# Attention's two products in plain float32, two small matmuls side by side in the array, in a one-core kernel of attention and two MoE layers

## The chip, the core and the metric

One NeuronCore of one Trainium2 chip runs the whole program in one launch. TensorE is called PE below (PEld is its weight load), VectorE DVE, ScalarE ACT, GpSimd POOL, and SyncE SP; SP issues nearly all transfers. The metric is the device time of one execution in microseconds (us), smaller is better, as the median of three runs.

## What is computed

Inputs are float32. Attention has 4 batches of 8 heads, 576 positions and 64 numbers a head; its output, 4 x 576 x 512, goes through two layers of a gated kind.

```python
def _attn_ref(q, k, v, s):
    scores = scale * np.matmul(q, k.transpose(0, 1, 3, 2))
    s_pos = np.maximum(s, 0.0)
    cum = np.cumsum(s_pos, axis=-1)
    bias = -(cum[:, :, :, None] - cum[:, :, None, :])
    scores = np.where(causal, -1000000000.0, scores + np.minimum(bias, 0.0))
    scores = scores - np.max(scores, axis=-1, keepdims=True)
    attn = np.exp(scores)
    attn = attn / (np.sum(attn, axis=-1, keepdims=True) + 1e-09)
    return np.matmul(attn, v).astype(np.float32)
...
x = attn_out.transpose(0, 2, 1, 3).reshape(B, S, H * D)
x = _moe_ref(x=x, **moe_kwargs)        # two products with w_in, a norm, one over positions with w_sg, one with w_out
return _moe2_ref(x=x, **moe2_kwargs)   # the same with other weights, relu in place of gelu, and no residual
```

## The kernel before

**Two number formats.** A float32 matmul has two forms here. The plain form is issued as two matmuls of all its columns. The other, float32r in the program and `fp32r` in the profile's rows where it is written, is one matmul, but with a rounded operand; to keep precision the kernel splits an operand into a rounded high part and the rest as a low part, and adds the products of the parts. The MoE layers (`plan_moe`, lines 284 to 523) work in parts throughout, and the change leaves them alone.

**Attention of a pair of heads** (two heads share 128 partitions, 64 each). `ldqk` loads q and k, `transposes` (lines 588 to 612) transposes them on PE (lines 596, 597) and splits the result: ACT writes the high parts (lines 608, 610), DVE the low parts (lines 609, 611). `stack` (614 to 625) then copies parts between partitions by transfers on SP, so that one 128-row product holds two part products: for each head two transfers make `qk` (622, 623), one makes the rows of `own` (624), and one brings the cumulated bias (617).

**Attention of a head** (`plan_head`, from 637). Steps S0 to S4 make the scores of five blocks of queries, in six pieces of 64, 192, 320, 448, 288 and 288 columns; each piece is two float32r matmuls (665), one with `qk` and one with `own` (66 rows: a part product and the bias). DVE masks a piece and takes the row minimum (670), ACT takes the exponential and its sum (674). N0 and N1: POOL adds 1e-9 and takes the reciprocal (681, 682) and scales the blocks (181, a helper). X0 to X3: PE transposes the blocks, 15 matmuls a head (727); ACT writes the rounded high part (736), DVE the low part (737). V0 to V3: for each of eight pieces, 1,600 columns in all, the values' product with the high part and with the low part (756). F0 and F1: ACT and DVE add the two halves of the sum (767, 768).

Six of the 32 heads (those with a 1 in `FULL`, line 56) do the values' product in the plain form instead (754), without low parts and with 64 weight columns, and the first pair's scores are plain too (`NQ`, line 58).

**Order.** A `Plan` holds all steps with a place (a head's number plus an offset of a table such as `HEAD`, line 35) and the steps they come after; it emits the steps in order of place, and a scheduler sets the order on each engine at build time. Each engine runs its list in that order. In the first batch there is no MoE work yet; `keep_busy` (lines 139, 820) puts 80 matmuls on zeros into that stretch, whose results nobody reads. The second layer comes behind the last attention (`late`).

Of the kernel before, what the change touches and what calls it, by code (L numbers as in the profile page):

```python
# [30 lines left out]
PA, PM, XB, NA = 6, 2, 3, 0  # L31

PAIR = {"ldqk": -6.63, "ldv": -4.33, "T": -2.16, "K": -4.2}
PAIR0 = {"ldqk": -1.63, "ldv": 0.61, "T": -6.3, "K": -6.13}
HEAD = {"S0": -1.3, "S1": -5.8, "S2": -3.15, "N0": -7.58, "S3": -2.18, "S4": -0.16, "N1": -2.11, "vs": 0.99,
        "X0": 0.5, "V0": -2.31, "X1": 0.53, "V1": -2.26, "X2": 0.21, "F0": 1.5, "X3": 1.38, "V2": -10.3,
        "V3": -2.32, "F1": 0.25}
HEAD0 = {"S0": -5.47, "S1": -2.29, "S2": -0.96, "N0": 0.24, "S3": -0.61, "S4": -0.21, "N1": 0.61, "vs": 1.03,
         "X0": -0.04, "V0": -3.06, "X1": -1.37, "V1": -2.52, "X2": 1.1, "F0": 1.62, "X3": 1.21, "V2": -4.61,
         "V3": -1.47, "F1": 1.82}  # L40

MOE = {"Va": (1.47, 2.25), "Vb": (-5.19, 8.0), "Vc": (-11.42, 14.73), "U": (3.8, 4.73), "ZY": (6.72, 5.81)}
WEIGHT = {"wv": (-1.41, 2.86), "wu": (8.16, 1.39), "sg": (3.51, 5.66), "wo": (10.07, 5.02)}
MOE2 = {"Va": (-14.18, 0.19), "Vb": (6.98, 8.23), "Vc": (-0.41, 3.39), "U": (7.05, 7.22), "ZY": (6.41, 19.75)}
WEIGHT2 = {"wv": (-3.82, 8.35), "wu": (9.3, 7.45), "sg": (13.98, 11.05), "wo": (0.84, 2.8)}

MORE = {"t2": 10.21, "d2": 5.99, "sp": 2.89, "sp2": -7.16, "cut": 1.74, "xr": -19.84, "w0": 11, "wn": 20,
        "ws": -1.0, "wd": 0.4, "wk": 4}


ENG = {"n0": "PPP.", "n1": "PPP.", "vshi": "AAD.", "vslo": "PPD.", "wlo": "PPDP", "wmin": "DPPP", "whi": "ADDD",
       "xhi": "DDAA", "xlo": "PPPP", "xdh": "...A", "xdl": "PPPP", "vn": "...D", "vhi": "...D", "vlo": "...P",
       "ghi": "ADPA", "glo": "DPDP", "mu": "PDPD", "var": "PDPD", "xc": "DAA.", "rg": "...D", "tq": "ADD.",
       "tk": "DAD.", "fc": "DAD.", "vc": "DPD.", "vcl": "DPP.", "vdup": "ADA.", "rc": "PPP."}

FULL = "00000100110001000000000000110000"

NQ = 1


def fl(ap):
    return ap.bitcast(F32)
# [35 lines left out]
def attention_two_moe_kernel(  # L98
# [433 lines left out]
    raw_v = ap.tile([128, NB, 2, D], F32, name="raw_v")  # L532
    nc.gpsimd.memset(raw_v[64:128, NT], 0.0)
# [7 lines left out]
    mx = [ap.tile([128, NB], F32, name=f"mx{i}") for i in range(2)]  # L541
    sm_ = [ap.tile([128, NB], F32, name=f"sum{i}") for i in range(2)]
# [5 lines left out]
    own_ = [ap.tile([D + 2, 2, S], F32R, name=f"own{i}") for i in range(2)]  # L548
    for t in own_:
        nc.vector.memset(fl(t[0:D]), 0.0)  # L550
        nc.vector.memset(fl(t[D:, 0]), 1.0)

    def cumulate():
# [11 lines left out]
        for e in range(2):  # L565
            nc.sync.dma_start(out=fl(own_[e][D:, 1]), in_=fl(ch[e:e + 1]))
# [8 lines left out]
    def plan_pair(plan, n, st):  # L575

        b, j = divmod(n, H // 2)
        full = n < NQ

        def ldqk():  # L580

            st["qk4"] = ap.tile([128, 4 * S], F32, tag="qk4", name="qk4")

            r = st["qk4"][:, :(2 * NT + 1) * 2 * D].rearrange("p (t e d) -> p t e d", t=2 * NT + 1, e=2)
# [29 lines left out]
        def stack(e):  # L614
# [3 lines left out]
            if full:  # L618
                return
# [328 lines left out]
```

## Time and profile before

| what | us |
|---|---|
| median of 3 runs (724.37 to 726.17) | 724.9 |
| the profiled execution: device time | 725.51 |
| its span, first to last instruction | 723.7 |
| PE busy (94% of the span), DVE, POOL, ACT | 678.8, 447.8, 393.9, 386.5 |

The profile has the busy time of each engine, a row of tenths for 40 equal slices of the span, groups of instructions by line and shape, who waited for whom, and instructions in order of time. A matmul's length in it runs until its result is written and overlaps the next; what it costs in a dense run is the distance from its start to the next start. Stages below are by time from the span's start: stage 1, 0 to 125 us (the first eight heads and the first layer's weights), stage 2, 125 to 425 (attention with the first layer), stage 3, from 425 (the end of the first layer and the second).

### The profile page before, as it was taken

The numbers are of one execution on the slowest core, as the hardware profiler recorded it, in microseconds if no ns is written. First come the engines' busy times: TensorE is split into PE (matmuls) and PEld (weight loads), VectorE is DVE, ScalarE is ACT, GpSimd is POOL, SyncE is SP. The second block draws the span as 40 slices with busy tenths as digits, with TensorE's granted clock in tenths as the row PEclk, the third lists the DMA queues.
The fourth block names the chain that finished last, engine by engine and source line by source line (L and its number), as shares of the span: only waits on it lengthen the run. The fifth ranks groups of instructions, "written<-read, shape, count | busy, mean of one in ns | idle before, by whom it ended". The sixth has DMA issues, their size and how long they took to land.

```text
span 723.7 us, 13198 instructions
## 1 busy us (share of the span) xinstructions
PE 678.8 (94%) x4377; PEld 604.1 (83%) x4377; DVE 447.8 (62%) x1191; ACT 386.5 (53%) x1002; POOL 393.9 (54%) x601
## 2 busy tenths in 40 slices
PE   9887888898999998989999999989889999999997
PEld 4476767678889998989979998979888998988996
DVE  8876767788568887766976749985871202402111
ACT  3675557888655876655876544543442414313321
POOL 4754747876474794476563546586674416413211
PEclk9998778999999999999999999999999999999999
DMA  8567677755566465466466053435521001010011
GB/s 210 144 160 173 175 164 156 190 138 124 116 149 153 99 169 119 103 152 154 95 161 140 18 164 84 142 110 187 167 84 52 0 30 46 2 44 30 0 47 57
DMA packets 94396, 81.60 MB, mean 113 GB/s; under 512 B 64116, under 2 KB 72308, under 8 KB 94328
## 3 DMA queue, kind: packets, MB, share of 16 engines
q1 hardware_dynamic: 93128, 80.46, 44.3%
q8 instruction: 35, 0.57, 0.3%
q10 hardware_dynamic: 1200, 0.30, 0.2%
q14 instruction: 33, 0.27, 0.1%
HBM read 39.87 MB, written 14.30 MB: 75 GB/s over the span
## 4 chain that ended last, share of the span: by engine, by line
PE 45%; DMA 6%; DVE 6%; POOL 2%; issue 2%; ACT 1%; SPq 1%; DVEq 0%; POOLq 0%; ACTq 0%
DMA stage<-in_moe_w_in_dram 3%; PE pp L727 3%; PE acc L756 2%; PE s L665 2%; PE pb L472 2%; PE pb L432 2%; PE pb L431 2%; PE pb L430 2%; PE pb L473 2%; PE pb L474 2%; PE pm L404 2%; PE pb L325 1%; PE pb L328 1%; PE pb L326 1%; PE pm L406 1%
## 5 line engine op out<-in xcount | busy, mean ns | idle before, releaser
L674 ACT ACTIVATE p<-p,mx 128x320 f32<-128x320 f32 (+4 forms) x160 | 89.6, 561 | 29.7 <-DVE mx L670 28.8
L181 POOL TENSOR_SCALAR p<-p,sum 128x448 f32<-128x448 f32 (+4 forms) x160 | 90.1, 575 | 4.9
L441 POOL TENSOR_TENSOR g<-u,g 128x256 fp32r<-128x256 f32 (+1 forms) x40 | 32.0, 805 | 94.7 <-ACT g L174 89.5
L727 PE MATMUL pp<-idf,p 128*128 128x128 f32 x480 | 78.7, 286 | 4.7 <-POOL p L181 4.5
L670 DVE CUSTOM_DVE_ANT_0 p<-s,mask 128x320 f32<-128x320 f32 (+4 forms) x160 | 66.1, 421 | 20.6 <-PE s L665 17.1
L436 DVE TENSOR_TENSOR u<-u,pb 128x320 f32<-128x320 f32 (+1 forms) x33 | 14.6, 451 | 95.9 <-PE pb L435 95.9
L665 PE MATMUL s<-qk 128*64 128x64 f32 (+7 forms) x204 | 64.1, 351 | 7.8 <-DMA qk<-qk 3.4
L737 DVE TENSOR_TENSOR pl<-pp,ph 128x320 fp32r<-128x320 f32 (+1 forms) x104 | 58.0, 566 | 14.4 <-ACT ph L736 9.0
L727 PEld LDWEIGHTS pp<-idf,p 128*128 128x128 f32 x480 | 57.8, 145 | 10.4 <-POOL p L181 5.2
L736 ACT CAST ph<-pp 128x320 fp32r<-128x320 f32 (+1 forms) x104 | 49.5, 490 | 28.1 <-PE pp L727 21.2
L681 POOL TENSOR_SCALAR sum<-sum 128x3 f32<-128x3 f32 (+1 forms) x64 | 17.0, 266 | 73.6 <-ACT p L674 70.6
L665 PE MATMUL s<-own 66*64 66x64 f32 (+3 forms) x192 | 55.8, 311 | 0.0
L682 POOL TENSOR_TENSOR sum<-sum,minus_one 128x3 f32<-128x3 f32 (+1 forms) x64 | 53.9, 843 | 3.3
L665 PEld LDWEIGHTS s<-qk 128*128 128x128 f32 (+3 forms) x204 | 36.3, 190 | 13.9 <-issue 5.9
L756 PE MATMUL acc<-ph,vs 128*128 128x320 f32 (+1 forms) x208 | 42.9, 289 | 4.8 <-ACT ph L736 2.8
L756 PE MATMUL acc<-pl,vs 128*128 128x320 f32 (+1 forms) x208 | 44.4, 297 | 0.2
L279 POOL TENSOR_TENSOR xl<-x,xh 128x576 fp32r<-128x576 f32 x24 | 35.2, 1479 | 15.6 <-ACT xh L174 12.7
L756 PEld LDWEIGHTS acc<-ph,vs 128*128 128x128 f32 x208 | 34.8, 200 | 8.2 <-ACT ph L736 4.2
L430 PE MATMUL pb<-sgh,vh 128*128 128x320 f32 (+1 forms) x132 | 39.4, 299 | 0.0
L431 PE MATMUL pb<-sgl,vh 128*128 128x320 f32 (+1 forms) x132 | 39.3, 298 | 0.0
L174 ACT CAST g<-u 128x256 fp32r<-128x256 f32 (+1 forms) x40 | 16.9, 432 | 41.8 <-DVE u L436 41.8
L404 PE MATMUL pm<-xh,inh 128*128 128x320 f32 (+1 forms) x124 | 38.3, 309 | 0.7 <-DVE u L275 0.7
(270 smaller groups left out, 2285.7 us busy)
## 6 DMA issues: line engine op xcount, KB each, us to landing
qk<-qk SPq DMA_DIRECT2D x60, 288.0 KB
own<-qk SPq DMA_DIRECT2D x30, 288.0 KB
x_d<-x SPq DMA_DIRECT2D x16, 288.0 KB
x<-x_d SPq DMA_DIRECT2D x16, 288.0 KB
qk<-in_q_dram SPq DMA_DIRECT2D x32, 128.0 KB
stage<-in_moe_w_in_dram SPq DMA_DIRECT2D x8, 512.0 KB
raw_v<-in_v_dram SPq DMA_DIRECT2D x32, 128.0 KB
stage<-in_moe_w_in_dram SPq DMA_DIRECT2D x16, 256.0 KB
```

The lines of the kernel that those rows point to most:

```text
L181: e.tensor_scalar(t, t, by, 1.0, ALU.mult, ALU.mult)
L404: nc.tensor.matmul(pu, W["inh"][:, kk, f], xh[:, kk, c], start=(kk == 0), stop=False)
L430: nc.tensor.matmul(pz, vh[sb][:, f], W["sgh"][:, sb, c], start=(sb == 0), stop=False)
L431: nc.tensor.matmul(pz, vh[sb][:, f], W["sgl"][:, sb, c], start=False, stop=False)
L665: nc.tensor.matmul(pp, a[:, qc], c[:, kc], start=c is first[1], stop=c is not first[1])
L670: nc.vector.tensor_tensor_reduce(out=p, in0=pp, in1=mask[:m, d0 + kc.start:d0 + kc.stop], scale=-0.125, scalar=3e38 if j == 0 else mxt[:m, ...
L674: nc.scalar.activation(p, p, AF.Exp, bias=mxt[:m, i:i + 1], scale=-1.0, accum_out=smt[:m, i:i + 1])
L682: nc.gpsimd.tensor_tensor(smt[:, c], smt[:, c], minus_one[:, c], ALU.pow)
L727: nc.tensor.transpose(ps[:, w:w + 128], pt[qb][:, kb * 128:kb * 128 + 128], idr if qb == kb and kb else idf)
L736: nc.scalar.copy(hi[:, :w], ps[:, :w])
L737: nc.vector.tensor_tensor(lo[:, :w], ps[:, :w], fl(hi[:, :w]), ALU.subtract)
L756: nc.tensor.matmul(acc, st["vs"][:, kb].rearrange("p a d -> p (a d)"), (hi if part == "hi" else lo)[:, c0:c0 + w], start=first, stop=last)
```

## The change

Scores are plain float32 products of q and k as they come out of the transposes. The two heads of a pair are done in one step: head e uses the array's rows 64 e to 64 e + 63, so its matmul has 64 rows (`rows`), and the two heads write different banks. The bias comes as a further float32r matmul of 64 rows, `ones` with `bias`. There are no parts of q, k, the exponentials or v, and none of the part transfers; the bias rows are still loaded. The values' product is plain for all heads: 12 pieces, with 64 weight columns each, of which 768 columns go to partitions 0 to 63 of the sum (a = 0) and 832 to partitions 64 to 127 (a = 1). One copy follows each group of transposes, and two copies of 64 partitions take the finished sum. The reciprocal moves from POOL to DVE. There are three sets of blocks `pts` for the heads and two buffers of v, and transposes of a head are grouped otherwise (5, 4, 4, 2). The values are one step behind all four groups of transposes. `keep_busy` in the first batch has no matmuls (`wn` 0), and all places are new.

```diff
-MORE = {"t2": 10.21, "d2": 5.99, "sp": 2.89, "sp2": -7.16, "cut": 1.74, "xr": -19.84, "w0": 11, "wn": 20,
...
-FULL = "00000100110001000000000000110000"
-
-NQ = 1
...
+HEAD = {"S2": -2.88, "N0": -0.6, "S4": -1.75, "N1": -0.41, "X0": -0.3, "X1": 0.02, "X2": 0.4, "X3": 0.46,
...
+MORE = {"t2": 10.76, "d2": 6.25, "sp": 2.89, "sp2": -6.56, "cut": 1.6, "xr": -19.03, "w0": 11, "wn": 0,
...
+       "fd": "ADA.", "vc": "DPD.", "vcl": "PPD.", "vdup": "ADA.", "rc": "DDD.", "x0": "DAA.", "x1": "DDD.",
+       "x2": "AAA.", "x3": "DDD."}
...
-    for j in range(2):
+    for j in range(3):
...
+    ones = ap.tile([128, 128], F32R, name="ones")
+    bias = [ap.tile([128, S], F32R, name=f"bias{i}") for i in range(2)]
...
+                copy(key, phase, st["qk"][:, i, c], ps[i])
...
-        def stack(e):
...
-            nc.sync.dma_start(out=fl(t[:D]), in_=fl(parts[:, 0:3:2]))
-            nc.sync.dma_start(out=fl(t[D:]), in_=fl(parts[:, 1:3]))
-            nc.sync.dma_start(out=fl(own_[e][:D]), in_=fl(parts[:, 0:4:3]))
...
+        def scores(i):
...
+            for j, (a, c0, k0, w) in enumerate(PARTS[i]):
+                kc = slice(k0, k0 + w)
+
+                for e in range(2):
+                    rows = slice(D * e, D * e + D)
+                    nc.tensor.matmul(st[a, e][:m, c0:c0 + w], st["qk"][rows, 0, qc], st["qk"][rows, 1, kc], start=True, stop=False)
+                for e in range(2):
+                    rows = slice(D * e, D * e + D)
+                    nc.tensor.matmul(st[a, e][:m, c0:c0 + w], ones[rows, :m], bias[n % 2][rows, kc], start=False, stop=True)
...
+        plan.add(f"S2.{n}", t0 + head["S2"], lambda: [scores(i) for i in range(3)],
+                 [f"T{n}", f"K{n}", f"S4.{n - 1}", f"X3.{2 * n - 2}", f"X3.{2 * n - 3}"])
+        plan.add(f"S4.{n}", t0 + head["S4"], lambda: [scores(i) for i in range(3, NB)], [f"S2.{n}"])
...
+    USE = [(0, 0, 320, 0, 0, 0), (1, 192, 192, 0, 1, 0), (2, 64, 192, 1, 1, 0), (0, 320, 192, 1, 0, 128),
+           (1, 0, 64, 2, 0, 256), (1, 64, 64, 3, 1, 0), (1, 128, 64, 0, 0, 320), (2, 320, 192, 2, 1, 0),
+           (2, 0, 64, 1, 0, 320), (2, 256, 64, 2, 0, 320), (3, 64, 128, 3, 1, 64), (3, 0, 64, 4, 1, 128)]
...
-            nc.scalar.copy(hi[:, :w], ps[:, :w])
-            nc.vector.tensor_tensor(lo[:, :w], ps[:, :w], fl(hi[:, :w]), ALU.subtract)
-            st["x", i] = hi, lo
...
+            copy(f"x{i}", phase, st["x"][i], ps[:, :w])
+
+        def values():
+            st["acc"] = psa.tile([128, 512], F32, tag="a", name="acc")
+
+            for j, (i, c0, w, kb, a, a0) in enumerate(USE):
+                nc.tensor.matmul(st["acc"][64 * a:64 * a + 64, a0:a0 + w], raw_v[m % 2][:, kb, odd], st["x"][i][:, c0:c0 + w],
+                                 start=j in (0, 1), stop=j in (9, 11))
+
+        def finish():
+            x = x_t(h // 2)
+            copy("fc", phase, x[rows, :384], st["acc"][0:64, :384])
+            copy("fd", phase, x[rows, 384:], st["acc"][64:128, :192])
```

In the list of PE before, in the middle of stage 2, the values' product of one head ends and the scores of the next follow (`ph` and `pl` are the high and low parts, `vs` the parts of v; `s` a bank of scores):

```order
L756 MATMUL acc_2669<-pl,vs 128x192
L756 MATMUL acc_2669<-pl,vs 128x64
L756 MATMUL acc_2672<-pl,vs 128x256
L756 MATMUL acc_2672<-ph,vs 128x192
L756 MATMUL acc_2672<-ph,vs 128x64
L756 MATMUL acc_2672<-pl,vs 128x192
L756 MATMUL acc_2672<-pl,vs 128x64
L665 MATMUL s_2727<-qk 128x320
L665 MATMUL s_2727<-own_152 128x320
L665 MATMUL s_2722<-qk 128x448
L665 MATMUL s_2722<-own_152 128x448
```

In the list of PE of the changed kernel, the scores of a pair stand so (`s_1603`, `s_1567` and `s_1577` are the first head's banks, `s_1604`, `s_1568` and `s_1578` the second's; each plain matmul is one row here and two matmuls on the chip):

```order
L617 MATMUL s_1603<-qk 128x288
L620 MATMUL s_1603<-bias_167,ones 128x288
L617 MATMUL s_1604<-qk 128x288
L620 MATMUL s_1604<-bias_167,ones 128x288
L617 MATMUL s_1567<-qk 128x448
L620 MATMUL s_1567<-bias_167,ones 128x448
L617 MATMUL s_1568<-qk 128x448
L620 MATMUL s_1568<-bias_167,ones 128x448
L617 MATMUL s_1577<-qk 128x320
L620 MATMUL s_1577<-bias_167,ones 128x320
L617 MATMUL s_1578<-qk 128x320
L620 MATMUL s_1578<-bias_167,ones 128x320
```

At this place a head's plain product and its bias stand together, and the other head's two come behind them; in other pairs the two plain products stand together and the two biases behind them. The values of a head in the changed list of PE are one run between two groups of transposes (`pt` are the copied transposes):

```order
L688 MATMUL pp<-idf,p_2_139 128x128
L698 MATMUL acc<-pt,raw_v_121 64x320
L698 MATMUL acc<-pt,raw_v_121 64x192 x3
L698 MATMUL acc<-pt,raw_v_121 64x64 x3
L698 MATMUL acc<-pt,raw_v_121 64x192
L698 MATMUL acc<-pt,raw_v_121 64x64 x2
L698 MATMUL acc<-pt,raw_v_121 64x128
```

Over the whole list of PE, matmuls of 64 rows or with 64 weight columns in the plain form come in 100 unbroken runs of one shape in the changed kernel (33 of scores, 18 of the 64-column pieces of scores, 49 of values). Before there are about 25. On SP the list of a pair before is this, all from its first to its last part transfer (`qk_1188` holds the parts):

```order
L617 DMA own_151<-cum_d 2x576
L622 DMA qk<-qk_1188 64x2x576
L623 DMA qk<-qk_1188 64x1152
L624 DMA own_151<-qk_1188 64x2x576
L201 DMA stage<-in_moe_w_out_dram 128x1024
L617 DMA own_152<-cum_d 2x576
L622 DMA qk<-qk_1188 64x2x576
L623 DMA qk<-qk_1188 64x1152
L624 DMA own_152<-qk_1188 64x2x576
```

and after the change, with the loads that stand near it:

```order
L600 DMA bias_167<-cum_d 2x576 x2
L570 DMA raw_v_122<-in_v_dram 128x4x64
L196 DMA stage<-in_moe_w_out_dram 128x1024
L570 DMA raw<-in_q_dram 128x4x64 x2
L571 DMA raw<-in_q_dram 64x2x64
```

Six of the eight transfers of a pair are gone; the two of the bias remain.

## Rows read from the trace of the kernel before

**Rows 1.** The page's line of PE's busy time: us, share of the span, instructions.

```profile
PE 678.8 (94%) x4377; PEld 604.1 (83%) x4377; DVE 447.8 (62%) x1191; ACT 386.5 (53%) x1002; POOL 393.9 (54%) x601
```

**Rows 2.** By stage: PE, PEld, DVE, ACT, POOL busy (instructions), granted clock, DMA share, GB/s.

```profile
0.00:125.00 125.00, 106.87 (x577) 78.08 (x577) 91.78 (x242) 74.26 (x201) 74.29 (x131) 0.88 0.70 169
125.00:425.00 300.00, 285.36 (x2038) 263.47 (x2038) 226.56 (x647) 204.07 (x544) 186.17 (x304) 0.99 0.56 130
425.00:724.00 299.00, 286.55 (x1765) 262.51 (x1764) 129.42 (x303) 108.17 (x258) 133.44 (x166) 0.99 0.24 72
```

**Rows 3.** The same for line 142 alone (only PE, PEld), stage 1.

```profile
0.00:125.00 125.00, 24.80 (x91) 8.79 (x91) 0.88 0.70 169
```

**Rows 4.** DVE in order of time (start, us): last step of heads one and eight.

```profile
43.96 0.41 DVE L768 TENSOR_TENSOR x<-acc,x 64x256 f32<-64x256 f32 x1
...
124.50 0.43 DVE L768 TENSOR_TENSOR x<-acc,x 64x256 f32<-64x256 f32 x1
```

**Rows 5.** Columns as in rows 2: between those two steps, and one stretch in it.

```profile
44.00:124.50 80.50, 66.92 (x381) 55.71 (x381) 57.11 (x165) 50.61 (x143) 49.64 (x79) 0.81 0.68 159
...
62.00:66.00 4.00, 2.48 (x13) 2.49 (x13) 0.49 (x1) 0.52 (x2) 0.00 (x0) 0.50 1.01 226
```

**Rows 6.** PE in order of time (start, us); in brackets idle time before, what ended it.

```profile
63.52 0.61 PE L665 MATMUL s<-qk 128*64 128x64 f32 x2 [2.85 <-DMA qk<-qk]
```

**Rows 7.** PE in order of time: float32r passes in dense runs (weight rows*columns, columns streamed).

```profile
42.12 0.29 PE L665 MATMUL s<-qk 128*128 128x288 f32 x1
42.26 0.30 PE L665 MATMUL s<-own 66*128 66x288 f32 x1
...
147.17 0.37 PE L665 MATMUL s<-qk 128*128 128x448 f32 x1
147.38 0.36 PE L665 MATMUL s<-own 66*128 66x448 f32 x1
```

**Rows 8.** PE in order of time: the first pair's plain scores, one head alone.

```profile
20.63 1.02 PE L665 MATMUL s<-qk 64*128 64x448 f32 x2
21.57 0.47 PE L665 MATMUL s<-own 66*128 66x448 f32 x1
```

**Rows 9.** PE in narrow windows of time: the first pair's plain scores, both heads.

```profile
10.91 0.27 PE L665 MATMUL s<-qk 64*64 64x64 f32 x2
...
11.17 0.60 PE L665 MATMUL s<-qk 64*128 64x192 f32 x4
...
10.91 1.33 PE L665 MATMUL s<-qk 64*64 64x64 f32 x10
12.18 1.04 PE L142 MATMUL idle<-mask 128*128 128x512 bf16 x4
```

**Rows 10.** PE in order of time: a head's first plain values, and what stands around.

```profile
141.91 0.39 PE L326 MATMUL pm<-inl,xh 128*128 128x512 f32 x1
142.13 0.39 PE L328 MATMUL pm<-inh,xl 128*128 128x512 f32 x1
142.45 1.62 PE L754 MATMUL acc<-ph,vs 128*64 128x320 f32 x6
144.00 1.09 PE L727 MATMUL pp<-idf,p 128*128 128x128 f32 x8
```

**Rows 11.** Groups by line: xcount, busy us, mean ns, idle before and who ended it.

```profile
L670 DVE CUSTOM_DVE_ANT_0 p<-s,mask 128x320 f32<-128x320 f32 (+4 forms) x160 | 66.1, 421 | 20.6 <-PE s L665 17.1 <-POOL p L181 1.3 <-PE acc L756 0.5
...
L737 DVE TENSOR_TENSOR pl<-pp,ph 128x320 fp32r<-128x320 f32 (+1 forms) x104 | 58.0, 566 | 14.4 <-ACT ph L736 9.0 <-PE pp L727 2.2 <-PE acc L756 1.8
...
L682 POOL TENSOR_TENSOR sum<-sum,minus_one 128x3 f32<-128x3 f32 (+1 forms) x64 | 53.9, 843 | 3.3
...
L768 DVE TENSOR_TENSOR x<-acc,x 64x320 f32<-64x320 f32 (+1 forms) x52 | 23.3, 452 | 7.3 <-ACT x L767 6.5
...
L670 DVE CUSTOM_DVE_ANT_0 p<-s,mask,mx 128x288 f32<-128x288 f32 x32 | 16.3, 510 | 1.7 <-PE s L665 0.6
...
L670 DVE DVE_READ_ACCUMULATOR2_ANT mx<- 128x1 f32 (+1 forms) x192 | 15.2, 79 | 0.0
```

More of the change, by code (lines that the diff above doesn't have):

```diff
@@ L28 @@
 SIGN = -(1 << 31)
[L31 to L40, printed above, removed]
@@ L627, in plan_pair @@
-        t0, where = 2 * n, PAIR0 if b == 0 else PAIR
-        plan.add(f"ldqk{n}", t0 + where["ldqk"], ldqk, [f"K1.{n - 1}"])
-        plan.add(f"ldv{n}", t0 + where["ldv"], lambda: load(raw_v, v, b, j, raw_v[0:REM, NT]), [f"vs{2 * n - 1}"])
-        plan.add(f"T{n}", t0 + where["T"], transposes,
-                 [f"ldqk{n}", f"K1.{n - 1}"]
-                 + ([f"S{i}.{2 * n - 2}" for i in range(NB)] if full else []))
-        for e in range(2):
-            plan.add(f"K{e}.{n}", t0 + where["K"] if n else -100.0, lambda e=e: stack(e),
-                     [f"T{n}", f"K{1 - e}.{n - 1 + e}"] + [f"S{i}.{2 * n - 2 + e}" for i in range(NB)])
+            st["qk"] = ap.tile([128, 2, S], F32, tag="qk", bufs=2, name="qk")
@@ new lines, in plan_pair @@
+        t0, where, head = 2 * n, PAIR0 if b == 0 else PAIR, HEAD0 if b == 0 else HEAD
+        plan.add(f"ldqk{n}", t0 + where["ldqk"], ldqk, [f"T{n - 1}"])
+        plan.add(f"ldv{n}", t0 + where["ldv"],
+                 lambda: load(raw_v[n % 2], v, b, j, raw_v[n % 2][0:REM, NT]), [f"V3.{2 * n - 3}"])
+        plan.add(f"T{n}", t0 + where["T"], transposes, [f"ldqk{n}", f"S4.{n - 2}"])
+        plan.add(f"K{n}", t0 + where["K"], rows_of_bias, [f"S4.{n - 2}", f"K{n - 1}"])
+        plan.add(f"S2.{n}", t0 + head["S2"], lambda: [scores(i) for i in range(3)],
+                 [f"T{n}", f"K{n}", f"S4.{n - 1}", f"X3.{2 * n - 2}", f"X3.{2 * n - 3}"])
@@ L676, in plan_head @@
-        for i in range(NB):
-            step(f"S{i}", lambda i=i: scores(i), [f"K{odd}.{n // 2}"] + [f"X{j}.{n - 2}" for j in range(4)] + ([f"S{i - 1}.{n}"] if i else []))
+            plan.add(f"{name}.{n}", n + (HEAD0 if n < H else HEAD)[name], fn, after)
         def norm(c):
@@ L740, in values @@
-        def values(i):
-            if i < 2:
-                if n < NA:
-                    st["acc", i] = psm.tile([128, 512], F32, tag="m", name=f"acc{i}")
-                else:
-                    st["acc", i] = psa.tile([128, 512], F32, tag="a", name=f"acc{i}")
-            hi, lo = st["x", i]
-            parts = ["hi"] if full else ["hi", "lo"]
-            for part in parts:
-                for j, (kb, c0, w, a, a0) in enumerate(USE[i]):
-                    first = part == "hi" and (i, j) in ((0, 0), (1, 0))
-                    last = part == parts[-1] and (i, j) in ((2, 1), (3, 1))
-                    acc = st["acc", a][:, a0:a0 + w]
-                    if full:
-                        nc.tensor.matmul(acc[:D], fl(st["vs"][:, kb, 0]), fl(hi[:, c0:c0 + w]), start=first, stop=last)
-                    else:
-                        nc.tensor.matmul(acc, st["vs"][:, kb].rearrange("p a d -> p (a d)"),
-                                         (hi if part == "hi" else lo)[:, c0:c0 + w], start=first, stop=last)
```

196 lines of the change are left out of this document (70 added, 126 removed), and 8 rows, old and new, of tables (SEG, USE).

## The prediction

> **What bounds the kernel now.** I read the page's busy times first: PE is busy for 94% of the span, no other engine for more than 62% [rows 1]. A busy PE is not a PE at its peak, so I took the stages next. Stage 2 and stage 3 are PE's: 285.4 of 300 us and 286.6 of 299 [rows 2]. Stage 1 is not. PE shows 106.9 of 125 us there, but 24.8 of it are the matmuls on zeros [rows 3], which fill waits; so in 125 - 106.9 + 24.8 = 43 us PE had no work that counts. Nobody else is full either: between the ends of heads one and eight [rows 4] DVE, the fullest, is busy for 57.1 of 80.5 us, 71% [rows 5]. These seven heads take 11.5 us each, and it is a chain that sets this: PE waits 2.85 us for a transfer of parts at 63.5 us [rows 6], while in the 4 us around it DVE, ACT and POOL work half a microsecond or less and the DMA engines are full [rows 5].
>
> So two questions decide. How much PE time do the new products take, in stage 2 where PE is the bound? And how much shorter does the chain of a head become in stage 1?
>
> **PE's passes, priced.** The distance from start to start is the price. A float32r pass of 288 columns takes 0.14 us, one of 448 columns 0.21 [rows 7]; this is 0.42 to 0.44 ns a column and some 0.015 us more. A plain product of 448 columns is two matmuls and takes 0.94 us with a load and a change of shape [rows 8]; I take 0.83 ns a column for each of the two, which fits the values' 1,664 columns in 1.55 us [rows 10].
>
> Scores. Before, a head has 12 float32r passes with 3,200 columns: 1.5 us, 48 us for 32 heads. After, a pair has plain products of 1,600 columns for each head. If the two heads run side by side, a pair takes 2 x 1,600 x 0.83 ns = 2.67 us, and its bias passes another 0.75: 3.4 us, 55 us for 16 pairs. If not, 6.8 us, 109 us. The trace has this case: for the first pair four matmuls of 192 columns, two for each head, are over in 0.60 us [rows 9], where their streaming alone, one after the other, takes 4 x 0.16 = 0.64 us, and the first two matmuls of 64 columns are both done 0.27 us after the first starts. All ten with 64 to 288 columns take 1.27 us to the next start; one after the other they would stream 1.33 us and have three changes of shape on top. So side by side it is: **+7 us**.
>
> Values. Before, 26 heads have 16 float32r passes with 3,200 columns, 1.55 us a head, and 6 have the plain form at 1,600 x 2 x 0.83 ns = 2.67 us: 56 us. After, all 32 are plain. Two halves of columns side by side leave the longer, 832 x 2 x 0.83 ns = 1.39 us a head, 44 us: **-12 us**. One after the other it is 2.67 us a head, 85 us: +29. No row shows two halves of weight columns at once; the nearest is the halves of rows [rows 9], and I take that.
>
> Changes of shape. From a 512-column pass to plain values of 64 weight columns it is 0.32 us instead of 0.22, and the six matmuls behind it take 1.55 us to the next start for 1.39 us of streaming [rows 10]: about 0.26 us a visit, 0.3 with the slower first transpose behind it, which I estimate. The changed list has 100 such runs and the old one about 25: 75 x 0.3 = **+22 us**. Runs that are cut by other work leave the two heads out of step; I add 6 (0 to 12). The transposes of a head, 15, stay.
>
> Sum on PE: 7 - 12 + 22 + 6 = **+23 us** (17 to 29 while both pairs of halves run side by side). It lies in stages 1 and 2; where PE is the bound, it counts in full.
>
> The Trainium skill says against this, on the page "TensorE: Matmul & The Clock Gate", Part 3, The mechanism, that matmuls start and end strictly in program order. In the changed list one head's product and bias stand ahead of the other head's, so by that rule a second head could begin only when the first one's last pass has begun. The two heads' first matmuls in this trace start together, ahead of the second matmul of the first head if each product is issued whole [rows 9]; the rule would add what the second rival below has.
>
> **What leaves the other engines.** DVE loses the low parts, 58.0 us, and the sums of halves, 23.3 [rows 11]; it gets copies instead, three a head in the first batch, and the reciprocals. POOL loses the powers of line 682, 53.9 us. The copies are on ACT and DVE, about half a microsecond each by the means of lines 737 and 768. The reciprocals on DVE have no row: between 0.08 us (a read of the accumulator) and 0.84 us (POOL's) [rows 11]; I take 0.15 an instruction, four a head, so 19 us, on an engine that in stage 2 has 73 of 300 us free [rows 2]. On the chain of a head this takes away the second of two steps behind each group of transposes (0.57 us, four groups), one of two steps at the end (0.45), about 0.7 of each power, and the waits for part transfers; it adds that the values now start only when all four groups are copied.
>
> **Stage 1.** DVE needs 8.2 us a head in the stretch of rows 5 (57.1 / 7), weights included. I estimate that it loses a net 1.2, so 7.0 is the floor of the pace, and 11.5 is no gain. I take 9.5, DVE then at 74%, near the 71% of today. The changed list puts twelve heads ahead of the first layer's first matmuls, so 12 x 2 = **-24 us**; from 0 to -36, which leaves a few of the 43 us. The matmuls on zeros cost nothing now and give nothing when they go, as long as the clock stays up (third rival).
>
> **Stage 2.** PE's shown waits there are 14.6 us [rows 2]. With shorter lists on DVE, ACT and POOL I take **-10** (0 to -18, the clock's 1% with it). Stage 3 has no attention but the tail: 0. The part transfers there stand off PE's path except where the chain waits, which is in these two terms.
>
> **Sum.** 723.7 + 23 - 24 - 10 = 712.7 us of span. The profiled execution took 725.51, 1.8 more than its span, and is 0.6 above the median: 712.7 + 1.8 - 0.6 = **714 us**. Own range, from the ends of the terms: 690 to 730.
>
> **Rivals.**
> 1. *The halves of weight columns do not run side by side.* For: no row shows it, and it is the part that does not do what the change says. Against: the halves of rows do. Price: 2.67 - 1.39 = 1.28 us a head, 41 us: **755 us**, slower. It decides the sign from 0.35 us a head on.
> 2. *PE keeps the order of its list.* For: the rows of the changed list alternate head by head with the bias in between. Against: rows 9. Worked out with the passes above, values take 1.87 us a head (+15), scores 4.1 to 5.5 a pair (+12 to +33, I take 24): **753 us**.
> 3. *The clock.* It was granted at half, 1.2 GHz, in stage 1 for 0.19 x 80.5 / 0.5 = 31 us, for example where PE had waited for parts and had 2.48 of 4 us of work [rows 5]. With the zeros gone it may be half for most of the first twelve heads. A head's scores and transposes, 3.3 us, would take twice that; I estimate that 1.3 us a head come onto the chain: +16, **730 us**.
> 4. *The reduces set the pace of the scores.* A pair's scores are 3.4 us of PE, but DVE reads the banks for (66.1 + 16.3 + 15.2) / 16 = 6.1 us [rows 11]. Where nothing else stands in PE's list meanwhile, PE loses 2.7 us a pair. In the first six pairs nothing does: +16, **730 us**. The Trainium skill has this on the page "TensorEngine Tiling (Array Packing)", PSUM Bottleneck: tiles in the array speed up TensorE but not the reading of its banks. Rows 11 say that DVE's reading is the longer here; the skill puts no number on it.
> 5. *More relief.* The chain of stage 1 was the transfers more than I allow, and stage 2 closes its hidden gaps: stage 1 at -36, stage 2 at -22: **690 us**.
>
> **How the numbers follow.** Chances: the forecast 0.47, rival 1 0.14, rival 2 0.11, rival 3 0.07, rival 4 0.07, rival 5 0.14. The range that should hold it 8 times in 10 is 684 to 752: from rival 5 with the low end of PE's term to just under rivals 1 and 2, which hold most of what is left out. Under about 0.3% a measurement cannot tell a change here, that is 722.7 to 727.1. Faster: most of the forecast (0.41) and rival 5 (0.14), 0.55. Slower: rivals 1 and 2, some two thirds of 3 and 4 and a little of the forecast, 0.38. Same: 0.07.
>
> **What would show it.** Side by side: two matmuls of the new values that write different halves, or of the two heads' scores, start within some 0.01 us of each other, and a head's values last about 1.5 us, not 2.8. Changes of shape: 0.1 us before and after such a run. Stage 1: the eighth head ends near 108 us and not at 125; the granted clock there; DVE's share near 75%. The reduces: PE idle inside a pair's scores, released by DVE's line of the reduce. I am wrong if values take over 1.8 us a head, or if the twelfth head ends as late as 150 us.

## The result and the profile after

The changed kernel takes 707.72 us (median of 4 runs, 705.1 to 708.57) where the kernel before, timed again beside it, takes 724.63: the ratio is 0.9762, with an interval of 0.9727 to 0.9797. That is 17 us less; the forecast was 11 less, and its range was 684 to 752. The profiled execution has a span of 705.9 us.

The page's line of busy times, to be set beside [rows 1]:

```profile
PE 665.9 (94%) x4733; PEld 583.3 (83%) x4733; DVE 411.7 (58%) x1189; ACT 340.8 (48%) x877; POOL 316.0 (45%) x476
```

Stages 1 and 2, with the columns of [rows 2]; the third stretch lies between the ends of heads one and eight:

```profile
0.00:125.00 125.00, 101.23 (x802) 79.03 (x803) 105.45 (x337) 74.33 (x214) 68.59 (x126) 0.96 0.51 133
125.00:425.00 300.00, 293.24 (x2258) 255.07 (x2257) 189.08 (x582) 162.42 (x415) 123.38 (x201) 0.98 0.25 68
34.00:95.70 61.70, 50.60 (x432) 41.07 (x430) 56.72 (x163) 35.15 (x102) 41.14 (x55) 0.94 0.49 132
```

In stage 2 PE is free for 6.8 of 300 us, before for 14.6. In stage 1 DVE has taken over as the fullest engine: 56.72 of 61.70 us, 92%, where it had 71%. The clock in stage 1 is 0.96, higher than before (0.88), although the 80 matmuls on zeros are gone.

The last steps of heads one, eight and 32 on ACT, in order of time (start, us), to be set beside [rows 4]:

```profile
33.73 0.32 ACT L169 COPY x<-acc 64x192 f32<-64x192 f32 x1 [0.23 <-DVE x L169]
...
95.11 0.31 ACT L169 COPY x<-acc 64x192 f32<-64x192 f32 x1 [0.35 <-DVE x L169]
...
408.49 0.31 ACT L169 COPY x<-acc 64x192 f32<-64x192 f32 x1 [0.27 <-DVE x L169]
```

Head one ends at 34.05 us and not at 44.4, head eight at 95.4 and not at 124.9. The same step of head 32 before stands here:

```profile
427.93 0.43 DVE L768 TENSOR_TENSOR x<-acc,x 64x256 f32<-64x256 f32 x1
```

So attention is over 19.6 us earlier, and of the 29.5 us won by the eighth head the other 24 heads give back 10. From there to the end it takes 297 us, before 295: nothing is won behind attention. What PE does from the end of head eight to the end of the kernel, before and then after (columns as in [rows 2]):

```profile
124.90:723.70 598.80, 572.01 (x3802) 525.98 (x3800) 356.05 (x951) 312.34 (x803) 319.61 (x470) 0.99 0.40 101
95.40:705.90 610.50, 589.66 (x4146) 524.29 (x4144) 330.90 (x940) 286.83 (x724) 261.68 (x374) 0.99 0.24 69
```

In this stretch PE is busy for 17.7 us more and free for 6.0 us less.

**What PE does now.** A head's values in one unbroken run, then the three runs of one pair's scores (PE in order of time):

```profile
259.90 1.79 PE L698 MATMUL acc<-pt,raw_v 128*64 128x320 f32 x24
261.62 0.44 PE L688 MATMUL pp<-idf,p 128*128 128x128 f32 x2
...
324.91 0.33 PE L617 MATMUL s<-qk 64*64 64x64 f32 x4
...
325.25 0.57 PE L617 MATMUL s<-qk 64*128 64x192 f32 x4
...
325.85 0.42 PE L425 MATMUL pm<-sgh,vh 128*128 128x320 f32 x1
...
328.09 1.03 PE L617 MATMUL s<-qk 64*128 64x288 f32 x4
...
330.56 0.50 PE L320 MATMUL pm<-inh,xh 128*128 128x512 f32 x1
...
333.27 0.76 PE L617 MATMUL s<-qk 64*128 64x288 f32 x4
333.65 0.51 PE L620 MATMUL s<-bias,ones 64*128 64x288 f32 x2
334.09 0.49 PE L323 MATMUL pm<-inh,xl 128*128 128x512 f32 x1
```

The values take 261.62 - 259.90 = 1.72 us from their first start to the next other start. One after the other their 24 matmuls would stream 2.67, so both halves of weight columns are at work at once. In the scores, 333.27 to 334.09 holds four plain matmuls of 288 columns and two bias passes in 0.82 us, and 328.09 to 330.56 is 2.47 us; with 0.94 for the first pieces (324.91 to 325.85) this pair takes 4.2 us. It is one of the four shortest: the last eight pairs, from 154 us on, take 4.2 to 5.4 us, 4.5 on average, and the first eight 4.9 to 7.4, with waits in them. Of the 17 heads whose values are not cut by other work, 14 take 1.72 us.

### The profile page after: what moved, and what is told of

It reads as the page before. It is cut to its first block, busy times and chain, and to the rows that moved or that the text cites. A ratio compares the mean times of both kernels' runs of the same rounds, so it can differ in the third digit from the quotient of the medians.

```text
span 705.9 us, 13188 instructions
## 1 busy us (share of the span) xinstructions
PE 665.9 (94%) x4733; PEld 583.3 (83%) x4733; DVE 411.7 (58%) x1189; ACT 340.8 (48%) x877; POOL 316.0 (45%) x476
## 4 chain that ended last, share of the span: by engine, by line
PE 64%; DVE 12%; DMA 10%; ACT 5%; POOL 4%; issue 3%; SPq 2%; POOLq 0%; DVEq 0%; ACTq 0%
PE acc L698 6%; PE pp L688 6%; PE s L617 4%; DMA stage<-in_moe_w_in_dram 4%; PE pm L399 2%; PE pm L425 2%; PE pm L320 2%; PE pm L426 2%; PE pm L427 2%; PE pm L401 2%; PE pm L400 2%; PE pm L321 2%; PE pb L399 2%; PE pb L400 2%; PE pb L401 2%
## 5 line engine op out<-in xcount | busy, mean ns | idle before, releaser
L631 ACT ACTIVATE p<-p,mx 128x576 f32<-128x576 f32 (+4 forms) x160 | 88.3, 553 | 28.9 <-DVE mx L625 28.0
L617 PE MATMUL s<-qk 64*128 64x288 f32 (+4 forms) x384 | 71.8, 418 | 3.1 <-DVE pt L169 1.3
L698 PE MATMUL acc<-pt,raw_v 128*64 128x64 f32 (+3 forms) x768 | 66.1, 295 | 3.5 <-DVE mx L625 3.0
L698 PEld LDWEIGHTS acc<-pt,raw_v 128*64 128x64 f32 x768 | 52.6, 141 | 16.6 <-issue 4.9
L625 DVE CUSTOM_DVE_ANT_0 p<-s,mask 64x64 f32<-64x64 f32 (+4 forms) x160 | 60.6, 421 | 9.7 <-PE s L620 9.0
L620 PE MATMUL s<-bias,ones 64*64 64x64 f32 (+4 forms) x192 | 57.7, 474 | 0.1
L617 PEld LDWEIGHTS s<-qk 64*128 64x128 f32 (+1 forms) x384 | 41.9, 180 | 14.9 <-issue 4.1
L169 DVE COPY pt<-pp 128x384 f32<-128x384 f32 (+2 forms) x72 | 34.0, 476 | 10.5 <-PE pp L688 10.0
L399 PE MATMUL pm<-xh,inh 128*128 128x256 f32 (+1 forms) x124 | 38.5, 311 | 1.6 <-DVE u L270 0.9
L199 ACT ACTIVATE stage<-stage 128x256 f32<-128x256 f32 (+1 forms) x36 | 18.5, 514 | 40.4 <-DMA stage<-in_moe_w_in_dram 33.8
L425 PE MATMUL pm<-sgh,vh 128*128 128x256 f32 (+1 forms) x124 | 37.9, 306 | 0.0
```

Of the source, the lines that this page charges most:

```text
L169: (e.copy if e is nc.scalar else e.tensor_copy)(out_, in_)
L399: nc.tensor.matmul(pu, W["inh"][:, kk, f], xh[:, kk, c], start=(kk == 0), stop=False)
L425: nc.tensor.matmul(pz, vh[sb][:, f], W["sgh"][:, sb, c], start=(sb == 0), stop=False)
L617: nc.tensor.matmul(st[a, e][:m, c0:c0 + w], st["qk"][rows, 0, qc], st["qk"][rows, 1, kc], start=True, stop=False)
L620: nc.tensor.matmul(st[a, e][:m, c0:c0 + w], ones[rows, :m], bias[n % 2][rows, kc], start=False, stop=True)
L625: nc.vector.tensor_tensor_reduce(out=pts[g][i][:m, kc], in0=st[a, e][:m, c0:c0 + w], in1=mask[:m, d0 + k0:d0 + k0 + w], scale=-0.125, scal ...
```

## Experiments

**1. Are the halves side by side?** Two runs take the overlap away. The first sorts the pieces of the values by half:

```diff
-    USE = [(0, 0, 320, 0, 0, 0), (1, 192, 192, 0, 1, 0), (2, 64, 192, 1, 1, 0), (0, 320, 192, 1, 0, 128),
...
+    USE = [(0, 0, 320, 0, 0, 0), (0, 320, 192, 1, 0, 128), (1, 0, 64, 2, 0, 256), (1, 128, 64, 0, 0, 320),
...
-                                 start=j in (0, 1), stop=j in (9, 11))
+                                 start=j in (0, 6), stop=j in (5, 11))
```

> The changed kernel with the values' pieces in another order: first all 768 columns that go to partitions 0 to 63 of the sum, then all 832 that go to 64 to 127. Same matmuls, same result. My theory (two halves of weight columns run side by side, but only those that stand next to each other in PE's list): a head's values stream for 2.67 us and not for 1.39, +1.28 us a head; over all 32 heads +41, of which the heads of the first batch hide a part: 735 to 750 us. Rival (the halves do not overlap, the gain is from elsewhere): 708 us, and a head's values last as long as in the changed kernel.

The second puts both heads on one half of the rows:

```diff
-                    rows = slice(D * e, D * e + D)
+                    rows = slice(0, D)
...
-                    rows = slice(D * e, D * e + D)
+                    rows = slice(0, D)
```

> The changed kernel with both heads of a pair on the array's rows 0 to 63: the second head's scores are computed from the first head's q, k and bias, so its own scores are left out; the matmuls have the same shapes and numbers. My theory (row halves run side by side): a pair's plain passes and its bias passes, 3.3 us of streaming side by side, become 6.7, +3.3 us a pair, +53 us over 16 pairs, of which the first batch hides a part: 740 to 762 us. Rival (the second half starts early in the records but gains nothing): 708 us.

Measured, one execution each: 730.3 and 747.1 us, 22.6 and 39.4 above the changed kernel's median, beside 724.3 for the kernel before. The first is less than I expected. A head's values in the first run, and the middle run of a pair's scores in the second (PE in order of time):

```profile
291.85 2.79 PE L699 MATMUL acc<-pt,raw_v 128*64 128x320 f32 x24
294.57 0.66 PE L689 MATMUL pp<-idf,p 128*128 128x128 f32 x4
```

```profile
363.24 2.25 PE L617 MATMUL s<-qk 64*128 64x288 f32 x6
...
367.95 0.49 PE L320 MATMUL pm<-inh,xh 128*128 128x512 f32 x1
```

The values take 2.72 us in place of 1.72, the same piece of the scores 4.71 in place of 2.47. Both pairs of halves run side by side, and without that the change would have been no gain. What was off is the size: sorting costs 1.00 us a head and not 1.28, since side by side the values take 1.72 and not 1.39. And only matmuls that stand near each other in PE's list overlap: the same ones sorted by half take 2.72 us, where 2.67 is their streaming one after the other.

**2. What does a change of shape cost?** One more matmul in the middle of each head's values, once with 128 weight columns and once with 64:

```diff
+                if j == 5:
+                    nc.tensor.matmul(st["acc"][:, 448:512], idf, st["x"][0][:, :64], start=False, stop=False)
```

```diff
+                if j == 5:
+                    nc.tensor.matmul(st["acc"][64:128, 448:512], raw_v[m % 2][:, 0, odd], st["x"][0][:, :64], start=False, stop=False)
```

> The changed kernel with one more product in the middle of each head's values, 64 columns of plain float32 with 128 weight columns on the identity, into columns of the sum that nobody reads: a change of tile shape and back in each head. My forecast took 0.3 us a visit with its change back. With 0.11 us of streaming this is +0.4 us a head, +9 to +13 us: 716 to 721 us. Rival (a change of shape is free): +0.11 us a head, 708 to 711 us.

> As the run with one more product of 128 weight columns in each head's values, but with 64 weight columns, in the half that is at work there anyway: no change of tile shape. Both theories: at most +0.11 us a head, 706 to 711 us. The difference to the other run is the price of two changes of shape.

Measured, one execution each: 724.3 and 711.3 us, both above what I expected. An unbroken head of the first run, then of the second (PE in order of time; line 701 is the extra piece, two matmuls):

```profile
280.94 1.19 PE L698 MATMUL acc<-pt,raw_v 128*64 128x320 f32 x12
282.06 0.43 PE L701 MATMUL acc<-pt,idf 128*128 128x64 f32 x2
282.43 0.88 PE L698 MATMUL acc<-pt,raw_v 128*64 128x64 f32 x12
283.24 0.66 PE L688 MATMUL pp<-idf,p 128*128 128x128 f32 x4
```

```profile
287.64 1.08 PE L698 MATMUL acc<-pt,raw_v 128*64 128x320 f32 x10
288.46 0.28 PE L701 MATMUL acc<-pt,raw_v 128*64 128x64 f32 x2
288.55 0.88 PE L698 MATMUL acc<-pt,raw_v 128*64 128x64 f32 x14
289.36 0.66 PE L688 MATMUL pp<-idf,p 128*128 128x128 f32 x4
```

From its first start to the next other start the first head takes 2.30 us, the second 1.72, as without the extra piece. The small one fits into a half that was waiting and costs this head nothing; the 3.6 us by which its one execution stands above the changed kernel's median are not explained by it. The large one costs 0.57, of which 0.11 is streaming. The other 0.46 us are two changes of shape and the overlap lost at the cut: in its rows all twelve matmuls ahead start before it and the other twelve behind it. That is a change in the middle of packed matmuls; an ordinary visit to the small shape and back costs less (see the next section). The list has 84 visits (35 runs of scores, 49 of values).

The second run's rows show one thing more. Six pieces, twelve matmuls, stand ahead of the extra piece in the list, but only ten start before it: the fifth piece waits for its half, and the two pieces behind it start first in the other half. So starts can differ from the order of the list by a piece or two.

**3. The transfers.** The kernel before, without the six part transfers of a pair:

```diff
+            t = ap.tile([128, 2, S], F32R, tag="qk", bufs=2, name="qk")
+            st["s"] = t[:, 0], t[:, 1]
...
-                nc.scalar.copy(qk4[:, 2 * i, c], pi)
+                nc.scalar.copy(t[:, i, c], pi)
...
-            nc.sync.dma_start(out=fl(t[:D]), in_=fl(parts[:, 0:3:2]))
-            nc.sync.dma_start(out=fl(t[D:]), in_=fl(parts[:, 1:3]))
-            nc.sync.dma_start(out=fl(own_[e][:D]), in_=fl(parts[:, 0:4:3]))
```

> The kernel before without the six part transfers of a pair: ACT writes the high parts of q and k into one tile, and the scores of both heads read its 128 rows, so the low parts' products are left out and each head gets the sum of both heads' products; matmul shapes and numbers, low-part work on DVE and everything else stay. Theory (the waits for the transfers are a large part of the chain in stage 1): the eighth head ends 10 us or more before 124.9, the whole takes 705 to 716 us. Rival (the transfers only fill time in which the chain waits for DVE, ACT and POOL anyway): 722 to 726 us.

Measured: 703.75 us (703.24 to 707.94), a little below the range of the theory; ratio 0.9709 (0.9643 to 0.9776). The last steps of heads eight and 32 (DVE in order of time), and stages 1 and 2 (columns as above):

```profile
111.63 0.43 DVE L765 TENSOR_TENSOR x<-acc,x 64x256 f32<-64x256 f32 x1
...
404.67 0.43 DVE L765 TENSOR_TENSOR x<-acc,x 64x256 f32<-64x256 f32 x1
```

```profile
0.00:125.00 125.00, 106.95 (x638) 77.41 (x643) 101.16 (x272) 84.59 (x232) 87.75 (x153) 0.99 0.47 123
125.00:425.00 300.00, 294.79 (x2101) 274.69 (x2100) 236.10 (x660) 201.79 (x531) 182.15 (x305) 0.99 0.26 72
```

Head eight ends 12.9 us earlier, head 32 23.3 us, and the whole is 21 us shorter: without the transfers the kernel before gains as much as the whole change gives. With them go some waits for buffers, since a pair's high parts now have a tile and two buffers of their own; no run separates the two. DVE, ACT and POOL all do more in stage 1 than in [rows 2]. What the rest of the change (plain products, fewer copies, new places) gains or loses on top is not shown: 707.7 is 4 us above 703.75, but the executions of the two kernels overlap (705.1 to 708.57 against 703.24 to 707.94), and this run leaves products out.

**4. The zeros and the clock.** The kernel before without its 80 matmuls on zeros:

```diff
-MORE = {... "wn": 20,
+MORE = {... "wn": 0,
```

> The kernel before without the 80 matmuls on zeros in the first batch. Theory (they fill waits and cost nothing): the time stays within 2 us of before, 722 to 727, if the clock of stage 1 stays near 0.88. Rival (they held the clock up, or stood in the way): slower by 3 to 15 us with a lower granted clock in stage 1, or faster by up to 10.

Measured: 725.3 us, ratio 1.001 (0.9971 to 1.0049). Stage 1:

```profile
0.00:125.00 125.00, 100.15 (x502) 76.18 (x503) 91.23 (x246) 74.68 (x204) 75.96 (x132) 0.78 0.69 170
0.00:45.00 45.00, 36.82 (x127) 23.73 (x127) 34.15 (x76) 22.71 (x57) 23.66 (x51) 0.62 0.70 181
45.00:125.00 80.00, 63.33 (x379) 52.46 (x377) 57.08 (x171) 51.97 (x148) 52.31 (x81) 0.87 0.69 163
```

The granted clock of stage 1 falls from 0.88 to 0.78, so PE spends more of it at 1.2 GHz, and the time is the same. All of the fall is in the first 45 us, 0.62 where the kernel before has 1.00; from 45 to 125 us the clock is 0.87, where it was 0.81. Head one ends 1.6 us later than before (46.0), head eight 1.2 earlier (123.8). So a lower clock in the first 45 us cost nothing here; what a lower clock between heads one and eight would cost, this run does not show.

**5. Does DVE set the pace of stage 1 now?** Two runs relieve it, one by the reciprocals of the first batch, one by two copies:

```diff
-"rc": "DDD."
+"rc": "PDD."
```

> The changed kernel with the reciprocals of the first batch back on POOL. In the changed kernel's stage 1 DVE is busy for 56.0 of the 61 us from 35 to 96, and the reciprocals with the sum before them take 15.7 us of DVE in the first 125 us. Theory (DVE sets the pace of stage 1 now): DVE falls to about 80% there, the eighth head ends 4 to 8 us before 95.7, the whole takes 700 to 705 us. Rival (the chain of a head sets it; POOL's power is 0.84 us against DVE's 0.16): the eighth head ends later by 0.5 us a step, 708 to 716 us.

```diff
-"x1": "DDD.", ... "x3": "DDD."
+"x1": "ADD.", ... "x3": "ADD."
```

> The changed kernel with the copies of the second and fourth group of transposes of the first batch on ACT and not on DVE, some 0.5 and 0.33 us a head. Theory (DVE sets the pace of stage 1): 8 heads x 0.85 = 7 us less on DVE there, the eighth head ends 3 to 6 us earlier, the whole takes 702 to 706 us. Rival (ACT's exponentials are in the chain and are delayed by the copies): the same time or up to 5 us more, 707 to 713 us.

Measured: 720.5 us, ratio 0.9942 (0.9908 to 0.9976), and 709.6, ratio 0.9776 (0.9713 to 0.9839). Between 34 and 95.7 us, the first and the second run, and the end of head eight in the first:

```profile
34.00:95.70 61.70, 46.51 (x348) 36.16 (x350) 40.26 (x118) 29.26 (x85) 47.10 (x65) 0.85 0.41 112
```

```profile
34.00:95.70 61.70, 50.05 (x381) 40.96 (x383) 51.93 (x145) 36.55 (x109) 39.66 (x52) 0.86 0.45 120
```

```profile
107.93 0.31 ACT L169 COPY x<-acc 64x192 f32<-64x192 f32 x1 [3.10 <-DVE x L169]
```

DVE falls to 65% and 84%, and nothing is won. With the power back on POOL head eight ends at 108.2, 12.8 us later, and the whole is slower than the rival had it too; with the copies on ACT it ends at 98.7, 3.3 later. My theory fell: DVE is 92% busy, and relief of DVE alone does not shorten stage 1. Both runs hand the work to another engine of the same chain (POOL's power takes 0.84 us, ACT has the exponentials), so that the chain of a head sets the pace is argued from them and not shown by them alone. Why DVE is so full shows in the changed kernel's order of time (DVE and POOL, start, us):

```profile
31.33 0.68 DVE L202 SCALAR_TENSOR_TENSOR stage<-stage 128x512 int32<-128x512 int32 x1
...
34.09 1.50 DVE L673 TENSOR_SCALAR sum<-sum 128x2 f32<-128x2 f32 x1
34.30 1.26 POOL L204 TENSOR_TENSOR inl<-stage,inh 128x512 fp32r<-128x512 f32 x1
...
35.76 2.55 POOL L176 TENSOR_SCALAR p<-p,sum 64x64 f32<-64x64 f32 x5 [0.20 <-DVE sum L674]
35.90 2.95 DVE L202 SCALAR_TENSOR_TENSOR stage<-stage 128x512 int32<-128x512 int32 x1
```

An addition on two columns, 0.17 us by its median, lasts until POOL's instruction ends (34.30 + 1.26 = 35.56; 34.09 + 1.50 = 35.59). Of the 28 additions of line 673 in the first 125 us, eight take 0.57 us or more, and each of the eight ends 0.02 to 0.04 us behind an instruction of POOL. A conversion on line 202 that took 0.68 at 31.3 us takes 2.95 under five instructions of POOL. So part of DVE's busy time looks like waiting for POOL that the profile counts as work. It is not so for every instruction: the 28 reciprocals behind the additions stay at 0.16 us, and another conversion takes 0.67 under POOL at 57.3 us. One run takes that addition away, on top of experiment 7 below:

```diff
-                nc.vector.tensor_scalar(smt[:, c], smt[:, c], 1e-9, None, ALU.add)
```

> The kernel with float32r parts for the scores of batches two to four, and without the addition of 1e-9 ahead of the reciprocals (the sums of a row's exponentials are at least 1, where float32 does not show 1e-9). In the changed kernel that addition has a median of 0.17 us, but a mean of 0.41 in the first 125 us and up to 1.85: it lasted until POOL's instruction at that moment ended. Theory (it stands in the chain of a head, on DVE, twice a head): 0.8 us less a head in the first batch and less on DVE, so the eighth head ends 2 to 5 us earlier than in the run with parts alone and the whole takes 696 to 700 us. Rival (the wait for POOL only moves on to DVE's next instruction): 700 to 703 us.

Measured: 702.8 us, ratio 0.9705 (0.9671 to 0.974), beside 701.0 without the edit. Head eight ends at 94.65 us without the edit and at 94.63 with it. This run takes work from DVE and gives it to nobody, and nothing is won. The rival holds in part: in the first 125 us the additions had 9.1 us of DVE, without them DVE is busy for 4.5 us less (106.96 to 102.50), and the conversions of the weights (lines 198, 201, 202) take 3.2 us more. The very next instruction, the reciprocal, stays at 0.16.

**6. Order in PE's list.** Two runs move only that: each product with its own bias behind it, and another order of the values.

```diff
                     nc.tensor.matmul(st[a, e][:m, c0:c0 + w], st["qk"][rows, 0, qc], st["qk"][rows, 1, kc], start=True, stop=False)
-                for e in range(2):
-                    rows = slice(D * e, D * e + D)
                     nc.tensor.matmul(st[a, e][:m, c0:c0 + w], ones[rows, :m], bias[n % 2][rows, kc], start=False, stop=True)
```

> The changed kernel with each piece of the scores written head by head (product and bias of the one, then of the other); in PE's list 177 of 192 products are then followed by their own bias, in the changed kernel 102. In its trace a pair in that order takes 4.9 us (at 123.9 us) where a pair whose products stand together takes 4.2 in its three runs (from 339.5). Theory (a half waits while the other's bias stands ahead of it, but not longer than that): 75 more such products, 0.7 x 75 / 12 = +4 us at most, 708 to 712 us. Second rival of the prediction (PE keeps its list strictly): 1.5 us a pair more, for six pairs +9, 715 to 720 us.

(The two times named there are 11.4 us too late: counted from the span's start as all others here, they are 112.5 and 328.1 us.)

```diff
...
+    USE = [(2, 320, 192, 2, 1, 0), (3, 0, 64, 4, 1, 128), (0, 0, 320, 0, 0, 0), (3, 64, 128, 3, 1, 64), (2, 0, 64, 1, 0, 320), (2, 64, 192, 1, 1, 0), (1, 128, 64, 0, 0, 320), (0, 320, 192, 1, 0, 128), (2, 256, 64, 2, 0, 320), (1, 192, 192, 0, 1, 0), (1, 64, 64, 3, 1, 0), (1, 0, 64, 2, 0, 256)]
...
-                                 start=j in (0, 1), stop=j in (9, 11))
+                                 start=j in (0, 2), stop=j in (10, 11))
```

> The changed kernel with the 12 pieces of the values in another order, in which a piece for the one half of the sum follows one for the other more evenly, and the first needs the third group of transposes. In the changed kernel an unbroken head takes 1.72 us where the longer half streams 1.39. Theory (the rest is a half that waits for its turn in the list): 0.1 to 0.2 us less a head where PE is the bound, 703 to 707 us. Rival (the rest is the change of shape): 707 to 709 us, 1.72 us a head.

Measured: 715.2 us, ratio 0.9834 (0.9793 to 0.9875), and 707.8, ratio 0.9741 (0.9711 to 0.9772). PE with the scores head by head, the same middle run as above, and a head's values in the new order:

```profile
333.48 1.50 PE L617 MATMUL s<-qk 64*128 64x288 f32 x4
...
337.26 0.50 PE L320 MATMUL pm<-inh,xh 128*128 128x512 f32 x1
```

```profile
235.50 1.64 PE L696 MATMUL acc<-pt,raw_v 128*64 128x192 f32 x24
237.07 0.33 PE L686 MATMUL pp<-idf,p 128*128 128x128 f32 x1
```

The run of scores takes 3.78 us in place of 2.47, and the whole 7 us more by the medians, which is inside the price of the prediction's second rival and above mine; by the ratios it is 5 us, since the kernel before took 727.8 beside these two runs. So a half does wait when the other half's bias stands ahead of it. The changed kernel shows it too, in a pair whose list is head by head (start, us):

```profile
112.54 0.33 PE L617 MATMUL s<-qk 64*64 64x64 f32 x2
112.79 0.24 PE L620 MATMUL s<-bias,ones 64*64 64x64 f32 x1
112.96 0.33 PE L617 MATMUL s<-qk 64*64 64x64 f32 x2
```

The second head's product starts behind the first one's bias. The Trainium skill says on the page "TensorE: Matmul & The Clock Gate", Part 3, The mechanism, that matmuls start in program order; these rows agree, but the second run of experiment 2 does not, where a piece is overtaken. There all matmuls are plain, and here a float32r pass stands in between. Whether the half waits for its turn in the list or for the change of format was not tested. The values in the new order take 1.57 us in place of 1.72, as expected, and the time is the same: in this run head eight ended at 99.2 us, 3.8 later, which would use up the 0.15 us a head; that is argued.

**7. A version that beats both.** If the transfers are what counted, parts may stay as long as they need no transfer. In batches two to four the scores take three float32r passes of 64 rows a head:

```diff
...
+                for i_, (x, y) in enumerate(((st["qk"], st["qk"]),) if b == 0 else st["parts"]):
+                    for e in range(2):
+                        rows = slice(D * e, D * e + D)
+                        nc.tensor.matmul(st[a, e][:m, c0:c0 + w], x[rows, 0, qc], y[rows, 1, kc], start=i_ == 0, stop=False)
...
```

> The changed kernel with the scores of batches two to four in three float32r passes of 64 rows a head (high by high, high by low, low by high) in place of the plain product; the parts stay on the partitions where the transposes leave them, so there are no part transfers. ACT writes the high parts, DVE the low parts; there is one buffer of v and one of low parts. A pair's products then stream for 3 x 1,600 x 0.42 = 2.0 us side by side and not for 2.67: 0.65 us less a pair, 12 pairs. Theory (PE is the bound in stage 2, and a float32r pass of 64 rows costs what one of 128 does): 8 us less there, 698 to 703 us. Rival (the low parts on DVE and the single buffers bring waits, or the passes cost more side by side): 706 to 715 us.

Measured: 701.0 us (699.39 to 701.96), ratio 0.9644 (0.961 to 0.9678), below the interval of the changed kernel. The 448 columns of both heads (PE in order of time; `lo` holds the low parts):

```profile
320.48 0.48 PE L629 MATMUL s<-qk 64*128 64x448 f32 x2
320.68 0.48 PE L629 MATMUL s<-lo,qk 64*128 64x448 f32 x2
320.89 0.48 PE L629 MATMUL s<-qk,lo 64*128 64x448 f32 x2
321.09 0.49 PE L632 MATMUL s<-bias,ones 64*128 64x448 f32 x2
321.29 0.43 PE L629 MATMUL s<-qk 64*128 64x320 f32 x2
```

Each of the first four lines holds both heads' passes and takes 0.20 us, about what one pass of 128 rows took in [rows 7]. The shortest pairs take 3.73 us and not 4.22, which would be 0.49 x 12 = 6 us of the 6.7 measured; but over the last eight pairs the mean falls from 4.51 to 4.26, which would be 3 us. How much of the rest is PE's passes stays open.

## Why the prediction came out as it did

The sign, the range and the two questions held; the size was short by 6 us. Up to the end of head eight the kernel is 29.5 us shorter, where the sum had 24 for stage 1, over twelve heads. From there on PE is busy for 17.7 us more, where the sum had 23, and free for 6.0 us less, where it had 10. The first two errors add up, and the third takes 4 us back: that the total is near is in part luck.

**PE's passes: about right.** Some 5 of the 17.7 us are work of the first layer that before stood ahead of head eight's end (18 matmuls at 0.22 us and ten transposes of weights), so 24 heads cost about 13 us more; the sum's 23 for 32 heads is 17 for 24. The share of the first eight heads, 6 us, went into the sum although PE is not the bound there. A visit costs what was taken: in the order of experiment 6 the values take 1.57 us, and their first start comes 0.09 us late (235.50, where the transpose ahead started at 235.30 and transposes stand 0.11 apart), so 1.57 + 0.09 - 1.39 = 0.27 us. In the changed kernel's own order the values take 0.15 us more, for which the sum had only the 6 us of runs out of step. There are 84 visits and not 100, since most 64-column pieces of the scores stand inside another run.

**Side by side: right, and it decides.** Rival 1 fell with experiment 1. Had it held, the run with sorted values says 730 us, so its 755 was too dear as well: part of it is hidden in stage 1, and the values were never at 1.39.

**Stage 1: the term that was too small.** The prediction moved only the pace, 11.5 to 9.5 us a head, and put the end of head eight near 108. The pace became (95.4 - 34.05) / 7 = 8.8, and head one ends 10 us earlier, of which the sum had nothing. These 10 us are not the transfers (the run without them: 42.2 us), not the zeros (46.0 without them) and not the reciprocals (33.8 with them on POOL). The new places and the shorter lists of a head are left; no run separates them. The twelfth head ends at 130.2 us, where 150 would have been a sign of being wrong; before it ended at 176.9, with work of the first layer ahead of it.

**Where the relief comes from.** The prediction named the part transfers among four causes. Experiment 3 makes them the largest one known: without them the span is 21.7 us shorter, where the whole change takes 29.5 us from the time to head eight and 6.0 from PE's waits behind it. In stage 1 alone they are 12.9 of the 29.5, and the pace is 10.0 us without them. How the rest divides between the shorter lists of DVE, ACT and POOL and the new places stays open, and no run puts the transfers back into the changed kernel.

**Stage 2: right in kind.** PE's free time fell from 14.6 to 6.8 us, where I took 10 off.

**Rival 2** is a mechanism of this kernel, not a mistake: order costs 1.3 us in one run of scores. In the changed kernel's list 80 of the 96 products of the first eight pairs stand right before their own bias, and these pairs take 4.9 us or more; their scores all begin before 130 us, where PE is mostly not the bound. In the last eight pairs it is 22 of 96. That this is why the rival did not decide is argued. I set it aside on [rows 9], where each head's passes are plain alone and no bias stands between.

**Rival 3** did not come: the clock rose in the changed kernel, and in the kernel before it fell in the first 45 us and cost nothing. (Not all of the 24.8 us of [rows 3] are the 80 matmuls: 11 more on zeros at the start, 4.5 us in the changed kernel, stay.) **Rival 4**: DVE is fuller than the 75% I named, but the runs that relieve it gain nothing. Its busy share had misled me in either direction, as part of it looks like a wait for POOL. In the first 125 us PE's waits for the reduces (line 625) come to 3.4 us, where the rival had 16. **Rival 5** had the direction: stage 1 lies between the forecast's 24 and its 36, but PE's waits fell by 6 us and not by its 22.

## What to carry to other kernels

Before changing the arithmetic to be rid of a data movement, take the movement alone away and see what is left: here that gained as much as the whole change, and parts that need no transfer gained more. Two small matmuls in different halves of the array are worth their place only near each other in the list, and each visit to another tile shape costs 0.3 to 0.5 us here. An engine that is 92% busy is not the bound until relieving it gains time.

## What the runs showed of the hardware

- Halves of weight columns run side by side as halves of rows do: 1.72 us against 2.72 for the same matmuls sorted by half.
- Two matmuls of 64 weight columns in a half that is idle cost the head nothing (1.72 us with and without), two of 128 in the same place 0.57.
- A piece of the values whose half is busy can be overtaken by one that stands behind it: ten of twelve matmuls start ahead of the extra piece.
- Some instructions of DVE between buffers in SBUF last until POOL's instruction beside them ends (0.17 became 1.50 us, 0.68 became 2.95); the reciprocals stay at 0.16.
